# Small value and key-value products of twelve units moved ahead of the next unit's scores in one run, and the masked scores kept in the gate tiles

## The chip, the cores and the metric

One core of a Trainium2 chip runs the whole program. The metric is device time in microseconds, the median of three executions, lower is better. A profile of one execution gives the rows that are read here.

## The reference, cut to what matters

Gated linear attention over 4 batches, 8 heads, 768 positions and 48 channels a head, followed by two feed-forward blocks:

```
f = sigmoid(f_logit)
state = f[t][:, None] * state + outer(k[t], v[t])     # for each batch and head, t = 0..767
y[t]  = q[t] @ state
x  = y.reshape(3072, 384)
xn = x / sqrt(mean(x*x) + 1e-6) * rms_g
x  = (silu(xn @ w_gate) * (xn @ w_val)) @ w_out       # 384 -> 1536 -> 384
out = relu(x @ w_in)**2 @ w_out2                      # 384 -> 2048 -> 384
```

## The kernel before, in words

The time axis is cut into 6 chunks of 128 positions; a chunk of one batch is a **unit**, 24 in all, numbered chunk by chunk, and four units make a **group** of 512 tokens. For each unit VectorE scans the gates from both ends (`scan_b`, `scan_a`), scales k and q by them (`mul_k`, `mul_q`), and TensorE forms the `scores` (k against q, 8 products of 64 rows, into PSUM banks `pa` and `pb`). VectorE masks them (`masked`), TensorE adds the state's part and the masked scores times v into the unit's output y (`attend`, 24 small products), and multiplies k by v (`kv`, 8 small products, not for the last chunk). VectorE adds that to the state of the batch (`state_add`); ScalarE has scaled the state by the chunk's gates (`decay`). k is transposed through DRAM (`k_turn`, `k_back`, `kcopy`), y is normalised (`norm`, `power`, `x_scale`), transposed through DRAM (`x_turn`, `x_back`) and split into a rounded and a remainder half (`x_high`, `x_low`).

The first feed-forward block works on a group at a time in 12 steps. A step has three blocks of 9 large products each of 128x512: G (gate), V (value, into bank `vv`) and O (the output product of the step before, called pending). In between ScalarE makes the silu (`sg`) and the rounded hidden half (`hh`), VectorE multiplies by V and makes the remainder (`hl`). The program is one written order: a step is cut into three **segments**, numbered 3f, 3f+1, 3f+2 in a group of 36. Segment 3f stands after G, 3f+1 after V, 3f+2 after O. In each segment first the functions in `side` are issued (VectorE, ScalarE and DMA work), then the step's own silu, multiplication or remainder, then the functions in `tail` (small TensorE products). Each engine takes its instructions in this order, and SyncE issues all transfers in it.

`plan_unit(u, s)` puts the parts of unit u at segments counted from s, the segment of its scores: `attend` at s + 2, `kv` at s + 6, `mul_q` at s itself. Units 8 to 23 are planned so; the first 8 stand in an order written out by hand. Work on the second block's weights (word operations on VectorE, rounded and remainder halves) is put by a planner into segments where its table of costs finds room; the `room` of a segment grows with the small products in it.

TensorE's banks are eight: `acc0` to `acc2` for O, `g`, `vv`, and `pa`, `pb`, `pc`. Before the change y goes to `pa`, the key-value product to `pb`, the masked scores into tiles of their own (`sm`).

Of the kernel before, what the change touches and what calls it, by code (L numbers as in the profile page):

```python
# [8 lines left out]
F32 = mybir.dt.float32  # L9
# [7 lines left out]
P = 128  # L17
B, H, S, D = 4, 8, 768, 48
C = 128
NCH = S // C  # L20
NPAIR = H // 2
DM = H * D
KT = DM // P
# [4 lines left out]
UG = 4  # L28
# [161 lines left out]
def tile_linear_attention_moe(  # L190
# [11 lines left out]
    nc = tc.nc  # L202
# [4 lines left out]
    def pool(name, stack=main, **kw):  # L207
        return stack.enter_context(tc.tile_pool(name=name, **kw))

    ps = pool("ps", bufs=1, space=PSUM)  # L210
# [5 lines left out]
    ap_ = pool("attn", upper, bufs=2, reuse_waits="tile")  # L216

    units = [(c, b) for c in range(NCH) for b in range(B)]
    NU = len(units) // UG
# [6 lines left out]
    mask = cp.tile([P, C], F32, name="mask")  # L226
# [26 lines left out]
    def flat(x):  # L253
        return x.rearrange("p a t -> p (a t)")


    U = {}
# [74 lines left out]
    def banks(u):  # L332
        return ("pa", "pb", "pc") if u >= UG or u % 2 == 0 else ("acc0", "acc1", "acc2")
# [41 lines left out]
    BL = 4  # L375

    def block_view(x, n):
        return flat(x)[:, 0:BL * n * 32].rearrange("p (b n j) -> p b n j", b=BL, n=n)

    def block_write(u, nm, t):  # L380
        n = t.shape[2]
        U[u][nm] = tc.dram_tile([P, BL, n, 32], F32, name=f"{nm}{u}")
        nc.sync.dma_start(U[u][nm], t)

    def block_read(u, nm, to):
        src = U[u][nm].rearrange("(a i) c n j -> c i a (n j)", a=BL)
        for c in range(BL):
            nc.sync.dma_start(to[32 * c:32 * c + 32].rearrange("i a n j -> i a (n j)"), src[c])
        U[u][nm + "o"] = to
# [15 lines left out]
        U[u]["xg"] = xg  # L405

    def x_turn(u):
        t = block_view(U[u]["q"], KT)
        nc.vector.transpose(
            t.rearrange("p a k i -> p k a i"), U[u]["xg"].rearrange("p (k a j) -> p k a j", k=KT, a=BL),  # L410
        )
        block_write(u, "xd", t)

    def x_back(u):
        block_read(u, "xd", ap_.tile([P, BL, KT, 32], F32, tag="sm", name=f"xo{u}", bufs=4))

    def x_part(t, u):
        return t[:, :, u % UG * C:(u % UG + 1) * C].rearrange("p k (c i) -> p k c i", c=BL)
# [21 lines left out]

    def attend(u):
        c, b = units[u]
        y = ps.tile([P, DM], F32, tag=banks(u)[0], name=f"y{u}")
        sub = [True, True]
        if c:
            for p in range(NPAIR):
                for i in range(2):
                    o = slice(64 * i, 64 * i + 64)
                    nc.tensor.matmul(
                        y[o, p * 2 * D:(p + 1) * 2 * D], U[u]["q"][:, p, o], state[b][:, p],  # L450
                        start=sub[i], stop=False, skip_group_check=True,
                    )
                    sub[i] = False
        for hf in range(2):
            sm = U[u]["sm", hf]
            for j in range(4):
                h = 2 * j + hf
                hs = slice(h * D, (h + 1) * D)
                for i in range(2):
                    o = slice(64 * i, 64 * i + 64)  # L460
                    nc.tensor.matmul(
                        y[o, hs], sm[:, j, o], U[u]["v"][:, hs],
                        start=sub[i], stop=True, skip_group_check=True,
                    )
                    sub[i] = False
        U[u]["y"] = y

    def kv(u):
        c, b = units[u]
        if c == NCH - 1:  # L470
            return
        kvp = ps.tile([P, NPAIR, D], F32, tag=banks(u)[1], name=f"kv{u}")
        for p in range(NPAIR):
            for o in (0, 64):
                h = 2 * p + o // 64
                nc.tensor.matmul(
                    kvp[o:o + D, p], U[u]["ktok"][:, p, o:o + D], U[u]["v"][:, h * D:(h + 1) * D],
                    start=True, stop=True,
                )
        U[u]["kv"] = kvp  # L480
# [269 lines left out]
    side, tail, planned, room = {}, {}, {}, {}  # L750
    TAIL = dict(scores=0.9, attend=1.3, kv=0.3)

    def at(where, s, fn):
        where.setdefault(max(s, NG), []).append(fn)

    starts = {}

    def plan_unit(u, s):
        starts[u] = s
        for k, fns in (  # L760
            (-9, (load_gates,)), (max(-9, starts.get(u - 2, 0) + 7 - s), (load_v,)),
            (max(-9, starts.get(u - 2, 0) + 9 - s), (load_qk,)),
            (-5, (gate,)), (-3, (scan_b, keep_end)), (-1, (scan_a, mul_k)),
            (0, (mul_q, k_turn, decay)), (1, (masked,)), (2, (k_back,)), (3, (norm, power)), (4, (x_scale,)),
            (5, (x_turn, kcopy)), (6, (x_back,)), (7, (state_add,)), (10, (x_high, x_low)),
        ):
            for fn in fns:
                if fn not in (load_gates, load_qk, load_v) or u > 2 * UG:
                    at(side, s + k, lambda fn=fn: fn(u))
                    planned.setdefault(s + k, []).append(fn.__name__)  # L770
        for k, fn in ((0, scores), (2, attend), (6, kv)):
            at(tail, s + k, lambda fn=fn: fn(u))
            room[s + k] = room.get(s + k, 0) + TAIL[fn.__name__]

    NG = 3 * F1
    for gi in range(1, NU - 1):
        for j in range(UG):
            plan_unit((gi + 1) * UG + j, gi * NG + ((4, 11, 18, 24) if gi == 1 else (-3, 6, 15, 24))[j])
    COST = dict(
        scan_b=(1.4, 0), keep_end=(0, 0.2), scan_a=(1.2, 0), mul_k=(0.7, 0), mul_q=(0.7, 0), masked=(1.4, 0),  # L780
        k_turn=(0.7, 0), kcopy=(0, 0.6), gate=(0, 2.2), decay=(0, 1.5), norm=(0, 1.0), x_scale=(0.6, 0), x_turn=(0.6, 0),
        state_add=(0.7, 0), x_high=(0, 0.5), x_low=(0.55, 0),
    )
# [149 lines left out]
    def piece(kind, i):  # L933
# [20 lines left out]
    unit_piece = dict(  # L954
        ld=load_unit, sb=scan_b, en=keep_end, sa=scan_a, mk=mul_k, mq=mul_q, sc=scores, kt=ktrans, kc=kcopy,
        y=attend, kv=kv, de=decay, st=state_add, no=norm, pw=power, nr=norm2, xt=xtrans, xh=xhigh, xl=xlow,
    )
    pair_piece = dict(wl=wload, ws=wscale, wb=wbits_low, wc=wbits_sign, wh=whigh, wz=wlow)
# [469 lines left out]
```

## Time and profile before

| what | before |
|---|---|
| median of 3 runs | 947.48 us (947.04 to 948.22) |
| the profiled execution | 947.26 us, of which the span 945.4 us |
| TensorE busy | 921.7 us, 97% of the span, 5945 products |
| VectorE busy | 644.3 us, 68% |
| ScalarE busy | 487.9 us, 52% |
| share of TensorE in the chain that ended last | 91% |

The span is the time from the first to the last instruction of the profiled execution. A busy TensorE is not one at its peak: the ends of its products are modelled and overlap, so what a stretch costs is read from the start times of its instructions.

### The profile page before, as it was taken

What the parts mean: (1) busy time and instruction counts of PE and PEld (TensorE: products, weight loads), DVE (VectorE), ACT (ScalarE), POOL (GpSimd) and SP (SyncE); (2) the same over time, 40 slices, a digit from 0 to 9 for tenths busy, and PEclk for the clock granted to TensorE, in tenths of its full rate; (3) what the DMA queues carried; (4) which work ended last, traced back from release to release, by engine and by line L of the source; (5) the groups of instructions that cost most, each with busy time, mean ns of one, the idle gap of its engine ahead of it and who ended that gap; (6) DMA issues with size and microseconds to landing.
All of it is one profiled execution on the core that took longest, in us unless ns stands there. A gap on an engine that the chain in (4) does not pass through costs nothing.

```text
span 945.4 us, 15739 instructions
## 1 busy us (share of the span) xinstructions
PE 921.7 (97%) x5945; PEld 810.1 (86%) x5945; DVE 644.3 (68%) x1147; ACT 487.9 (52%) x1020; POOL 31.1 (3%) x54
## 2 busy tenths in 40 slices
PE   7799999989999999999999999999999999999997
PEld 4578887878787888878888889999999999999997
DVE  7899968666767877767754636756775676666552
ACT  6877654545444545444433425556546554655551
POOL 3210000000000000000000000000000000000000
PEclk8999999999999999999999999999999999999999
DMA  9455424565556566545237257540754065305300
GB/s 335 165 202 193 178 86 166 160 193 168 161 163 198 182 202 191 185 151 196 106 121 245 74 196 269 183 149 9 242 160 134 15 228 167 126 25 185 117 26 29
DMA packets 78387, 148.48 MB, mean 157 GB/s; under 512 B 17248, under 2 KB 44000, under 8 KB 78304
## 3 DMA queue, kind: packets, MB, share of 16 engines
q1 hardware_dynamic: 78304, 147.39, 47.3%
q8 instruction: 49, 0.80, 0.4%
q14 instruction: 34, 0.28, 0.1%
HBM read 115.12 MB, written 32.24 MB: 156 GB/s over the span
## 4 chain that ended last, share of the span: by engine, by line
PE 91%; DMA 3%; DVE 2%; ACT 2%; issue 1%; SPq 0%; POOL 0%; DVEq 0%; POOLq 0%; ACTq 0%
PE o L730 7%; PE o L728 7%; PE o L729 7%; PE X L1104 7%; PE Y L1104 6%; PE v L728 5%; PE g L728 5%; PE acc L728 5%; PE acc L729 5%; PE acc L730 5%; PE v L730 5%; PE v L729 5%; PE g L730 5%; PE g L729 5%; PE T L1104 2%; PE R L1104 2%
## 5 line engine op out<-in xcount | busy, mean ns | idle before, releaser
L730 PE MATMUL o<-wb,h 128*128 128x384 f32 x384 | 128.6, 335 | 0.0
L729 PE MATMUL o<-wb,h 128*128 128x384 f32 x384 | 128.3, 334 | 0.0
L728 PE MATMUL o<-wb,h 128*128 128x384 f32 x384 | 128.3, 334 | 0.0
L975 ACT CAST hh<-sg 128x512 fp32r<-128x512 f32 x72 | 44.7, 620 | 110.0 <-DVE sg L972 108.8
L972 DVE TENSOR_TENSOR sg<-v,sg 128x512 f32<-128x512 f32 x72 | 49.6, 688 | 61.6 <-PE v L730 61.5
L1104 PE MATMUL X<-xc,wa 128*128 128x384 f32 x360 | 82.4, 336 | 0.0
L730 PEld LDWEIGHTS o<-wb,h 128*128 128x128 f32 x384 | 72.1, 188 | 0.5
L728 PEld LDWEIGHTS o<-wb,h 128*128 128x128 f32 x384 | 72.1, 188 | 0.0
L729 PEld LDWEIGHTS o<-wb,h 128*128 128x128 f32 x384 | 72.1, 188 | 0.0
L967 ACT ACTIVATE sg<-g 128x512 f32<-128x512 f32 x72 | 42.8, 594 | 54.2 <-PE g L730 53.9
L1104 PE MATMUL Y<-xc,wa 128*128 128x384 f32 x300 | 68.3, 335 | 0.0
L1104 PEld LDWEIGHTS X<-xc,wa 128*128 128x128 f32 x360 | 63.7, 188 | 1.8 <-ACT d L1179 1.2
L1183 DVE TENSOR_TENSOR c<-T,c 128x384 f32<-128x384 f32 x40 | 22.3, 558 | 52.4 <-PE T L1104 43.3
L977 DVE TENSOR_TENSOR hl<-sg,hh 128x512 fp32r<-128x512 f32 x72 | 49.3, 685 | 9.8 <-ACT hh L975 9.8
L1104 PEld LDWEIGHTS Y<-xc,wa 128*128 128x128 f32 x300 | 53.3, 188 | 0.7 <-DVE c L1183 0.6
L1134 DVE TENSOR_TENSOR h<-d,h 128x384 fp32r<-128x384 f32 x60 | 32.8, 554 | 26.2 <-ACT h L1133 26.2
L1133 ACT CAST h<-d 128x384 fp32r<-128x384 f32 x60 | 30.2, 511 | 34.4 <-PE o L730 34.4
L1179 ACT COPY d<-X 128x384 f32<-128x384 f32 x40 | 19.1, 478 | 54.7 <-PE X L1104 54.7
L728 PE MATMUL g<-xh,wh_o 128*128 128x512 f32 x108 | 43.1, 399 | 0.8 <-ACT sg L967 0.8
L728 PE MATMUL v<-xh,wh_g 128*128 128x512 f32 x108 | 43.8, 406 | 0.0
L728 PE MATMUL v<-xh,wh_v 128*128 128x512 f32 x108 | 43.4, 402 | 0.1
L728 PE MATMUL g<-xh,wh_g 128*128 128x512 f32 x108 | 43.2, 400 | 0.0
(192 smaller groups left out, 2237.5 us busy)
## 6 DMA issues: line engine op xcount, KB each, us to landing
wa<-w2d_c SPq DMA_DIRECT2D x100, 384.0 KB, 3.3
raw<-in_w_dram SPq DMA_DIRECT2D x18, 768.0 KB, 4.3
ff<-in_ff_dram SPq DMA_DIRECT2D x20, 516.0 KB, 5.3
qk<-in_qk_dram SPq DMA_DIRECT2D x20, 512.0 KB, 6.4
w2d_c<-ws_c SPq DMA_DIRECT2D x50, 192.0 KB, 2.7
raw_a<-in_w_dram SPq DMA_DIRECT2D x22, 384.0 KB, 4.2
wb<-w2d_b SPq DMA_DIRECT2D x16, 384.0 KB, 3.7
v<-in_vp_dram SPq DMA_DIRECT2D x24, 192.0 KB, 5.6
```

Of the source, the lines that this page charges most:

```text
L728: nc.tensor.matmul(o, lh, rh, start=first, stop=False)
L729: nc.tensor.matmul(o, lh, rl, start=False, stop=False)
L730: nc.tensor.matmul(o, ll, rh, start=False, stop=last)
L967: nc.scalar.activation(dd["s", f], dd["g", f], AF.Silu)
L972: nc.vector.tensor_mul(dd["s", f], dd["v", f], dd["s", f])
L975: nc.scalar.copy(dd["h", f][0], dd["s", f])
L977: nc.vector.tensor_sub(dd["h", f][1], dd["s", f], dd["h", f][0].bitcast(F32))
L1104: nc.tensor.matmul(o, w[a], x[:, b], start=first and n == 0, stop=last and n == 2, skip_group_check=True,)
L1133: nc.scalar.copy(t[:, 0], r)
L1134: later(lambda: nc.vector.tensor_sub(t[:, 1], r, t[:, 0].bitcast(F32)))
L1179: nc.scalar.copy(t, bk[b])
L1183: nc.vector.tensor_add(t, bk[b], t)
```

## The change

For units 12 to 23 `attend` and `kv` leave their own places and stand at e, the segment of the next unit's scores, ahead of these: one run of small products (attend, kv, scores of the next unit) where three stood apart. e is nine segments after s; the first segments of the units move a little so that each e is one that follows O (3f+2). The output y goes to bank `pc` (units 8 and on), the key-value product to `pc` for units 8 to 11 and to `vv`, the bank of the value block, from unit 12 on. The masked scores of units 12 and on are written over the unit's two gate tiles (`r` one segment after the scores, `f` three after), so the next load into these waits for `attend`. `x_turn` writes into a tile of its own, and `mul_q` and `mul_k` stand one segment ahead of the scores for all planned units, `scan_a` two. Work after `attend` (norm, scale, turn) moves with it.

```
-        t = block_view(U[u]["q"], KT)
+        t = ap_.tile([P, BL, KT, 32], F32, tag="xn", name=f"xt{u}")
...
+    def mask_into(u, hf, x):
+        sm = flat(x)[:, 0:4 * C].rearrange("p (j t) -> p j t", j=4)
+        nc.vector.tensor_mul(sm, U[u]["sc", hf], mask.unsqueeze(1).broadcast_to([P, 4, C]))
+        U[u]["sm", hf] = sm
+    def mask_r(u):
+        mask_into(u, 0, U[u]["r"])
+    def mask_f(u):
+        mask_into(u, 1, U[u]["f"])
...
-        y = ps.tile([P, DM], F32, tag=banks(u)[0], name=f"y{u}")
+        y = ps.tile([P, DM], F32, tag="pc" if u >= 2 * UG else banks(u)[0], name=f"y{u}")
...
-        kvp = ps.tile([P, NPAIR, D], F32, tag=banks(u)[1], name=f"kv{u}")
+        kvp = ps.tile([P, NPAIR, D], F32, tag="vv" if u >= 3 * UG else "pc" if u >= 2 * UG else banks(u)[1], name=f"kv{u}")
...
+    def plan_unit(u, s, e=None):
+        far = e is not None
+        y, b = (e, e + 1) if far else (s + 2, s + 3)
+        kv_at, back = (e, e + 4) if far else (s + 6, s + 6)
+        g = -5 if far else -6
+        end = e + 8 if far else s + 10
+        for n, at_ in zip(("gates", "qk", "v"), (e + 1,) * 3 if far else (s + 4, s + 6, s + 7)):
+            free[n, u] = at_
+        plan = [
+            (max(s - 10, free.get(("gates", u - 2), 0)), (load_gates,)),
+            (max(s - 9, free.get(("v", u - 2), 0)), (load_v,)),
+            (max(s - 9, free.get(("qk", u - 2), 0)), (load_qk,)),
+            (s + g, (gate,)), (s + g + 2, (scan_b, keep_end)), (s - 2, (scan_a,)), (s - 1, (mul_k, mul_q)),
+            (s, (k_turn, decay)), (s + 1, (mask_r,) if far else (masked,)), (s + 2, (k_back,)),
+            (s + 3, (mask_f,) if far else ()), (s + 5, (kcopy,)), (kv_at + 1, (state_add,)),
+            (b, (norm, power)), (b + 1, (x_scale,)), (b + 2, (x_turn,)), (back, (x_back,)), (end, (x_high, x_low)),
+        ]
...
-        for k, fn in ((0, scores), (2, attend), (6, kv)):
-            at(tail, s + k, lambda fn=fn: fn(u))
+        for k, fn in ((s, scores), (y, attend), (kv_at, kv)):
+            at(tail, k, lambda fn=fn: fn(u))
...
-            plan_unit((gi + 1) * UG + j, gi * NG + ((4, 11, 18, 24) if gi == 1 else (-3, 6, 15, 24))[j])
+    begin = [NG + x for x in (4, 11, 18, 24)]
+    for gi in range(2, NU - 1):
+        begin += [gi * NG + x for x in (-7 if gi == 2 else -10, -1, 8, 17)]
+    begin.append(begin[-1] + 9)
+    for n in range(len(begin) - 1):
+        plan_unit(2 * UG + n, begin[n], begin[n + 1] if n >= UG else None)
```

On TensorE, before, the small products of units 14 and 15 stand in three places. `y14` is unit 14's attend, `kv14` its key-value product, `sc15` the two score banks of unit 15; `acc`, `g` and `v` are large products of the feed-forward block:

```order
L730 MATMUL acc_2_2_2593<-hh_2_4_2815,wl_o4_891 128x512
L449 MATMUL y14_2910<-state2_99,qk14_2628 64x96 x8
L461 MATMUL y14_2910<-v14_2626,sm14_0_2883 64x48 x8
L461 MATMUL y14_2910<-v14_2626,sm14_1_2885 64x48 x8
L728 MATMUL g_2_6_2935<-xh_1_2_1876,wh_g6_969 128x512
...
L476 MATMUL kv14_3023<-v14_2626,ktok14_2988 48x48 x8
L728 MATMUL v_2_7_3032<-xh_1_2_1876,wh_v7_1055 128x512
...
L341 MATMUL sc15_0_3094<-qk15_2852 128x128
L341 MATMUL sc15_1_3095<-qk15_2852 128x128
```

On TensorE, after the change, the same products of units 14 and 15 (the two rows of scores come four times):

```order
L741 MATMUL acc_2_2_2626<-hh_2_4_2844,wl_o4_891 128x512
L460 MATMUL y14_2912<-state2_99,qk14_2527 64x96 x8
L472 MATMUL y14_2912<-v14_2525,ff14_2523 64x48 x16
L487 MATMUL kv14_2937<-v14_2525,ktok14_2837 48x48 x8
L341 MATMUL sc15_0_2946<-qk15_2765 128x128
L341 MATMUL sc15_1_2947<-qk15_2765 128x128
...
L739 MATMUL g_2_6_2956<-xh_1_2_1877,wh_g6_969 128x512
```

They have moved into one run between O and the next G; of the four borders with large products that the second and the third place had, none is left.

On TensorE, before, around the key-value product of unit 10 and the scores of unit 11, which stand together in both programs, with the engines whose semaphores they wait for:

```order
L476 MATMUL kv10_2161<-v10_1783,ktok10_2117 48x48 [waits PE_49,Activation_49]
L476 MATMUL kv10_2161<-v10_1783,ktok10_2117 48x48 x7
L341 MATMUL sc11_0_2170<-qk11_2032 128x128 [waits DMAHW3_49,DVE_49,PE_49]
L341 MATMUL sc11_1_2171<-qk11_2032 128x128 [waits DVE_49,PE_49]
L341 MATMUL sc11_0_2170<-qk11_2032 128x128
```

On TensorE, after the change, at the same place:

```order
L487 MATMUL kv10_2151<-v10_1785,ktok10_2114 48x48 [waits DVE_49,Activation_49]
L487 MATMUL kv10_2151<-v10_1785,ktok10_2114 48x48 x7
L341 MATMUL sc11_0_2160<-qk11_1954 128x128 [waits DMAHW5_49,DVE_49]
L341 MATMUL sc11_1_2161<-qk11_1954 128x128
L341 MATMUL sc11_0_2160<-qk11_1954 128x128
```

The order is the same, but the key-value product now lies in `pc`, and the second bank of scores (`sc11_1`) waits for VectorE and for TensorE no longer.

On VectorE, before, between the state addition of unit 14 and the transposition of unit 15's k (L319 is `mul_k`, L322 `mul_q`, L316 `scan_a`, L395 `k_turn`, `sg` the product with V, `hl` the remainder):

```order
L492 TENSOR_TENSOR state2_99<-kv14_3023,state2_99 48x4x48 x2
L665 TENSOR_TENSOR ws_c1_3_2995<-ws_c1_3_2995 128x384
L972 TENSOR_TENSOR sg_2_7_3021<-v_2_7_3032,sg_2_7_3021 128x512
L316 SCALAR_TENSOR_TENSOR ff15_2848<-ff15_2848,seed_90 128x516
L319 TENSOR_TENSOR qk15_2852<-qk15_2852,ff15_2848 128x512
L977 TENSOR_TENSOR hl_2_7_3054<-sg_2_7_3021,hh_2_7_3053 128x512
L322 TENSOR_TENSOR qk15_2852<-qk15_2852,ff15_2848 128x512
L395 STREAM_TRANSPOSE ff15_2848<-qk15_2852 128x4x4x32
```

On VectorE, after the change, the same instructions:

```order
L319 TENSOR_TENSOR qk15_2765<-qk15_2765,ff15_2761 128x512
L322 TENSOR_TENSOR qk15_2765<-qk15_2765,ff15_2761 128x512
L995 TENSOR_TENSOR sg_2_5_2872<-v_2_5_2874,sg_2_5_2872 128x512
L395 STREAM_TRANSPOSE ff15_2761<-qk15_2765 128x4x4x32
L721 TENSOR_TENSOR ws_c1_0_2840<-m_a3_2654,ws_c1_0_2840 128x128
L721 TENSOR_TENSOR ws_c1_0_2840<-m_a3_2654 128x128
L1000 TENSOR_TENSOR hl_2_5_2890<-sg_2_5_2872,hh_2_5_2889 128x512
L503 TENSOR_TENSOR state2_99<-kv14_2937,state2_99 48x4x48 x2
L419 TENSOR_TENSOR ff15_2761<-sc15_0_2946,mask_88 128x512
```

`mul_q` has moved ahead of the product with V (`sg`) of the segment before the scores, and the state addition now stands behind the remainder `hl` and ahead of the mask of the next unit.

## Rows read from the trace of the kernel before

**Rows 1.** The page, part 1: busy time, share of the span, instructions

```profile
PE 921.7 (97%) x5945; PEld 810.1 (86%) x5945; DVE 644.3 (68%) x1147; ACT 487.9 (52%) x1020; POOL 31.1 (3%) x54
```

**Rows 2.** Windows, stretch of planned units: us, busy by engine, clock, DMA

```profile
133.00:490.00 357.00, 352.09 (x2499) 285.14 (x2498) 249.37 (x440) 172.20 (x357) 8.78 (x16) 1.00 0.54 173
```

**Rows 3.** Waits of TensorE, whole span: total us, times, longest

```profile
PE sc L341 <- PE g L730: 0.5, 2, 0.2
```

**Rows 4.** Timeline of TensorE, key-value product alone: start us, us, instruction

```profile
304.05 0.39 PE L730 MATMUL g<-xh,wl_g 128*128 128x512 f32 x1
...
305.20 0.39 PE L729 MATMUL v<-xl,wh_g 128*128 128x512 f32 x1
```

**Rows 5.** Timeline of TensorE, scores alone

```profile
310.89 0.39 PE L730 MATMUL g<-xh,wl_o 128*128 128x512 f32 x1
311.21 1.16 PE L341 MATMUL sc<-qk 64*128 64x128 f32 x16
...
312.64 0.39 PE L729 MATMUL v<-xl,wh_v 128*128 128x512 f32 x1
```

**Rows 6.** Timeline of TensorE, a block O and an attend alone

```profile
314.47 0.39 PE L728 MATMUL acc<-hh,wh_o 128*128 128x512 f32 x1
...
316.29 0.39 PE L730 MATMUL acc<-hh,wl_o 128*128 128x512 f32 x1
...
318.67 0.39 PE L729 MATMUL g<-xl,wh_g 128*128 128x512 f32 x1
```

**Rows 7.** Timeline of TensorE, unit 6's key-value product with unit 7's attend

```profile
118.20 0.39 PE L730 MATMUL v<-xh,wl_v 128*128 128x512 f32 x1
118.52 0.56 PE L476 MATMUL kv<-v,ktok 128*48 128x48 f32 x16
118.91 0.85 PE L449 MATMUL y<-state,qk 128*64 128x96 f32 x16
...
120.94 0.39 PE L729 MATMUL acc<-hl,wh_o 128*128 128x512 f32 x1
```

**Rows 8.** Timeline of TensorE, key-value product of unit 10, scores of unit 11

```profile
195.40 0.39 PE L730 MATMUL g<-xh,wl_g 128*128 128x512 f32 x1
195.72 0.56 PE L476 MATMUL kv<-v,ktok 128*48 128x48 f32 x16
196.21 0.49 PE L341 MATMUL sc<-qk 64*128 64x128 f32 x2
199.17 1.13 PE L341 MATMUL sc<-qk 64*128 64x128 f32 x14 [2.47 <-DVE state L492]
...
200.56 0.39 PE L729 MATMUL v<-xl,wh_g 128*128 128x512 f32 x1
```

**Rows 9.** Timeline of TensorE and VectorE, ahead of unit 21's scores

```profile
422.23 0.39 PE L730 MATMUL g<-xh,wl_g 128*128 128x512 f32 x1
...
423.16 0.69 DVE L322 TENSOR_TENSOR qk<-qk,ff 128x512 f32<-128x512 f32 x1
...
423.95 0.79 PE L341 MATMUL sc<-qk 64*128 64x128 f32 x9 [1.33 <-issue]
```

**Rows 10.** Groups of VectorE in 133 to 490 us: count, busy, mean ns

```profile
L972 DVE TENSOR_TENSOR sg<-v,sg 128x512 f32<-128x512 f32 x47 | 32.5, 691 | 38.4 <-PE v L730 38.3
...
L568 DVE SCALAR_TENSOR_TENSOR m_a<-raw_a,m_a 128x768 int32<-128x768 int32 x10 | 9.5, 953 | 0.3
...
L492 DVE TENSOR_TENSOR state<-kv,state 48x192 f32<-48x192 f32 x25 | 8.8, 353 | 2.2 <-PE kv L476 2.1
L395 DVE STREAM_TRANSPOSE ff<-qk 128x512 f32<-128x512 f32 x12 | 8.5, 712 | 0.4
```

**Rows 11.** Windows, behind small products early on, and behind rows 8

```profile
32.00:36.00 4.00, 4.00 (x27) 1.96 (x26) 3.97 (x8) 2.18 (x5) 0.88 (x2) 0.75 0.59 197
...
201.00:204.00 3.00, 3.00 (x15) 2.45 (x14) 1.13 (x2) 0.60 (x2) 0.00 (x0) 1.00 0.82 283
```

**Rows 12.** DMA issues: count, KB each, median us from issue to landing

```profile
ff<-in_ff_dram SPq DMA_DIRECT2D x20, 516.0 KB, 5.3
```

More of the change, by code (lines that the diff above doesn't have):

```diff
@@ L754, in at @@
         where.setdefault(max(s, NG), []).append(fn)
[L756 to L766, printed above, removed]
+    free = {}
@@ new lines, in plan_unit @@
+    def plan_unit(u, s, e=None):
[15 more added lines that the diff above has]
+        ]
+        for k, fns in plan:
@@ L767, in plan_unit @@
             for fn in fns:
                 if fn not in (load_gates, load_qk, load_v) or u > 2 * UG:
-                    at(side, s + k, lambda fn=fn: fn(u))
-                    planned.setdefault(s + k, []).append(fn.__name__)
-        for k, fn in ((0, scores), (2, attend), (6, kv)):
-            at(tail, s + k, lambda fn=fn: fn(u))
-            room[s + k] = room.get(s + k, 0) + TAIL[fn.__name__]
-    NG = 3 * F1
-    for gi in range(1, NU - 1):
-        for j in range(UG):
-            plan_unit((gi + 1) * UG + j, gi * NG + ((4, 11, 18, 24) if gi == 1 else (-3, 6, 15, 24))[j])
+                    at(side, k, lambda fn=fn: fn(u))
@@ new lines, in plan_unit @@
+                    planned.setdefault(k, []).append(fn.__name__)
+        for k, fn in ((s, scores), (y, attend), (kv_at, kv)):
+            at(tail, k, lambda fn=fn: fn(u))
+            room[k] = room.get(k, 0) + TAIL[fn.__name__]
+    NG = 3 * F1
+    begin = [NG + x for x in (4, 11, 18, 24)]
[4 more added lines that the diff above has]
+        plan_unit(2 * UG + n, begin[n], begin[n + 1] if n >= UG else None)
@@ L779, in tile_linear_attention_moe @@
     COST = dict(
-        scan_b=(1.4, 0), keep_end=(0, 0.2), scan_a=(1.2, 0), mul_k=(0.7, 0), mul_q=(0.7, 0), masked=(1.4, 0),
+        scan_b=(1.4, 0), keep_end=(0, 0.2), scan_a=(1.2, 0), mul_k=(0.7, 0), mul_q=(0.7, 0), masked=(1.4, 0), mask_r=(0.7, 0), mask_f=(0.7, 0),
         k_turn=(0.7, 0), kcopy=(0, 0.6), gate=(0, 2.2), decay=(0, 1.5), norm=(0, 1.0), x_scale=(0.6, 0), x_turn=(0.6, 0),
```

## The prediction, made before the changed kernel was run

> **What bounds the kernel now.** The page first: TensorE is busy 97% of the span, VectorE 68%, ScalarE 52% [rows 1]. So a change pays only where it takes time out of TensorE's own sequence, and costs only where it makes TensorE wait. The stretch that the change touches is that of the planned units, 133 to 490 us: TensorE shows 352.1 of 357.0 us busy there at a granted clock of 1.00, the 2.4 GHz level [rows 2]. That looks full, but busy ends are modelled, so I read start times. Eight steps inside one block O take 316.29 - 314.47 = 1.82 us, 0.2275 us a product, 2.05 us a block of nine [rows 6]. Around small products the steps are longer: from the last large product ahead of unit 15's scores to its first scores 311.21 - 310.89 = 0.32 us instead of 0.23 [rows 5]. A change between large and small products therefore costs something each way, and joining runs should save it.
>
> **What the change removes: borders.** I measure a run from the start of the last large product ahead of it to the start of the second large product behind it; two large steps (0.455 us) belong to the large work.
> - Attend alone: 318.67 - 316.29 = 2.38 us [rows 6]. Key-value product alone: 305.20 - 304.05 = 1.15 [rows 4]. Scores alone: 312.64 - 310.89 = 1.75 [rows 5].
> - One joined run exists already, unit 6's key-value product with unit 7's attend: 120.94 - 118.20 = 2.74 [rows 7]. Apart they take 2.38 + 1.15 - 0.455 = 3.075. **A join of these two saves 0.335 us.** Its attend begins 0.39 us after the key-value product did, with no hole between [rows 7]. After the change attend comes first; I take the same price, since both use all 128 rows of the array in both orders.
> - Scores behind a key-value product stand in one place, which then stalls [rows 8]. Up to the first scores it takes 196.21 - 195.40 = 0.81, and from the first scores on a free run takes 312.64 - 311.21 = 1.43 [rows 5]; joined without a stall 2.24, apart 1.15 + 1.75 - 0.455 = 2.445. **A join with scores behind saves 0.205 us.** No row shows scores behind an attend (units 20 to 22 have no key-value product); I take 0.205 there too.
> - Count: units 12 to 19 join attend and key-value product (8), the scores of units 13 to 23 stand behind another small product (11). 8 x 0.335 + 11 x 0.205 = 2.68 + 2.26 = **4.9 us**. Bounds: all 19 at 0.335 give 6.4; none worth anything gives 0.
>
> **What it removes: stalls.**
> - Unit 10's key-value product lies in bank `pb`, where unit 11's scores go next. Two scores issue, then TensorE waits 2.47 us for the state addition that reads the bank [rows 8]. With the product in `pc` the order shows no such wait. The run took 200.56 - 195.40 = 5.16 us against 2.24 free: **2.9 us**. Lower bound 0 if VectorE held it anyway; but `mul_q` of unit 11, the other thing the scores need, now stands a segment earlier.
> - `mul_q` stands in the same segment as the scores before. For unit 21 it starts at 423.16, takes 0.69, and the scores begin at 423.95, 1.72 us after the last large product instead of 0.32: 1.40 us lost, booked as "issue" but ended by `mul_q` [rows 9]. Two more scores waited 0.5 us in all the same way [rows 3]. After the change `mul_q` is issued ahead of the product with V, and between V's end and the scores TensorE has a block O and an attend, 2.05 + some 1.9 us: **1.9 us** saved, lower bound 0.
>
> **What it adds, at nothing, and what covers it.**
> - The value bank: from unit 12 the key-value product sits in `vv`, and the next V must wait for the state addition. From the start of the key-value product to V TensorE now has 0.49 (to the first scores), 1.43 and a block G of 2.05, some 4.0 us [rows 5, 6, 8]. In the worst row, with the transposition and weight work queued ahead, the addition let the scores go 199.17 - 195.72 = 3.45 us after the product began [rows 8]. Counted from V's end the longest queue that the order shows for these units is the product with V (0.69), the transposition (0.71), three word operations (0.95 at most each), the remainder (about 0.69) and two additions (0.35 each) [rows 10]: 5.7 us, against 2.05 for O, 3.4 for the joined run and 2.05 for G, 7.5. Room of 1.8 us, less what VectorE is late when V ends; nothing charged.
> - Masks in the gate tiles: the gates of unit u + 2 load only after attend of u, and ScalarE's sigmoid work on them stands three blocks later, 6.1 us [rows 6], against a median landing of 5.3 us [rows 12]. Should they land late, silu waits behind them on ScalarE, but the next G needs its bank only after V and O, 4.1 us later.
> - The turned x has its own tile, the second mask stands two segments later; both on VectorE, same count of instructions, off TensorE's path. Transfers are the same in number and size; SyncE's loads move behind attend.
> - The planner puts the weight work later. The last split of an input for the second block still stands ahead of three whole steps, some 18 us, so phase two starts as before.
>
> **Sum.** 4.9 + 2.9 + 1.9 = 9.7 us less. The profiled execution took 947.26 us, 0.22 below the median shown; 947.26 - 9.7 = 937.6. I predict **937.5 us**.
>
> **A rule against it.** The joined run of rows 7 shows weights of an attend following a key-value product on the same 128 rows without a hole, and 0.335 us saved. The Trainium skill, "TensorE: Matmul & The Clock Gate", section "The mechanism" in Part 3, says that a weight load overlaps products in flight only when their row groups differ. By that rule neither kind of join would run on without a pause, the joins would be worth nothing and the time 942.5. Rows 7 disagree for one of the two; no row settles attend followed by scores.
>
> **The rivals.**
> 1. *Joins worth nothing* (what a run costs follows its own loads, not its borders): only the stalls go, 947.3 - 4.8 = 942.5. For it: the scores' first steps stay slow behind a key-value product too (0.205 against 0.335). Against it: rows 7. Chance 0.09.
> 2. *The value bank becomes the wait, slower.* If V stood still for the state addition as the scores of unit 11 did, 2.47 us [rows 8] in each of 8 units, 19.8 us: 937.5 + 19.8 = 957.3. It eats the gain from 1.2 us a unit on, that is if the addition ends over 3 us later than the queue above says. For it: VectorE is the busiest engine after TensorE, 249 of 357 us [rows 2]. Against it: the two sums above. Chance 0.05.
> 3. *The clock.* A run of 3.4 us of small products leaves most of the array idle. After sparse small work early on the granted clock was 0.75 over 4 us, partly the 1.2 GHz level: 1.0 us lost [rows 11]. Eleven joined runs at that price: 948.5, no change. Against it: behind the key-value product, stall and scores of rows 8, some 4.5 us, the clock stayed 1.00 [rows 11]. Chance 0.04.
> 4. *Late gates or a crowded VectorE* hold the scores or the silu in part of the units: half of the gain gone, 942.5 to 945. For it: 5.3 us is only a median, and units 12 and 13 have two blocks, 4.1 us, instead of three [rows 6, 12]. Against it: 4.1 us of slack. Chance 0.07.
>
> **How the numbers follow.** The forecast has 0.75: from 935.0 (all joins at 0.335 give 936.1; another 1 us where ends of other small waits go) to 940. Taking in rival 1 and the lower half of rival 4 the range is 935.0 to 942.6, with about 0.84 of the chance. A measurement of this kernel tells about 0.2%, 1.9 us, from no change. Rivals 1 and 4 are still faster by more than that: faster 0.75 + 0.09 + 0.07 = 0.91; same 0.04, rival 3 with the edges; slower 0.05, rival 2.
>
> **What would show it.** In the profile after: joined runs of 2.38 + 1.15 + 1.75 - 2 x 0.455 - 0.335 - 0.205 = 3.83 us where attend, key-value product and scores stand together, and 3.47 where attend and scores alone do (2.38 + 1.75 - 0.455 - 0.205); unit 11's scores without a wait; scores of units 12 to 23 with no idle time ahead; V behind each joined run starting one step after G. Wrong would be: idle time ahead of V that the state addition ends, a clock below 1.00 after the joined runs, or ScalarE waiting for gates with G idle behind it.

## The result, and the profile after

| | before | after |
|---|---|---|
| median, five runs each, in turn on one chip | 947.48 us (947.04 to 950.25) | 938.55 us (937.19 to 939.01) |
| ratio, 95% interval | | 0.9897 [0.9881, 0.9914] |
| the profiled execution | 947.26 us, span 945.4 | 937.19 us, span 934.7 |

The kernel became 8.9 us faster by the medians, against 937.5 us predicted: the time lies 1.05 us above the number and inside the range. The page of the kernel after, part 1, answers to [rows 1]: 921.7 us of busy TensorE have become 915.9, with the same 5945 products.

```profile
PE 915.9 (98%) x5945; PEld 810.3 (87%) x5945; DVE 640.9 (69%) x1147; ACT 488.6 (52%) x1020; POOL 34.2 (4%) x54
```

The window over the planned units of the kernel after (us, busy by engine, clock, DMA share, GB/s) answers to [rows 2]. TensorE was idle for 4.9 of 357 us there, and is idle for 0.7 of 363 now. Busy ends are modelled, so this says where holes went and not what the borders gave.

```profile
121.00:484.00 363.00, 362.26 (x2583) 298.13 (x2582) 253.81 (x454) 178.23 (x368) 11.95 (x17) 1.00 0.53 166
```

**Where the time came from.** I cut both executions by start times on TensorE: an early part up to the first G of group 2, the planned stretch from there to the last V of the first block, and the rest. The two limits, in the timeline of the kernel before and then of the kernel after:

```profile
134.56 0.39 PE L728 MATMUL g<-xh,wh_g 128*128 128x512 f32 x1
...
564.20 0.39 PE L730 MATMUL v<-xh,wl_v 128*128 128x512 f32 x1
```

```profile
132.25 0.39 PE L739 MATMUL g<-xh,wh_g 128*128 128x512 f32 x1
...
553.12 0.39 PE L741 MATMUL v<-xh,wl_v 128*128 128x512 f32 x1
```

The planned stretch went from 564.20 - 134.56 = 429.64 to 553.12 - 132.25 = 420.87 us: **8.8 us**, nearly all of the difference of the medians. The early part, counted from the first product, is 133.1 us in the profiled execution before and 130.8 after; TensorE's order is the same there in both, and in the ten experiments below it lies anywhere from 130.3 to 133.5, in programs with the order of before (131.7 and 130.7 in the first two) as with that of after. It differs from execution to execution, so I compare kernels by the planned stretch, and by medians only beside it. The rest, from the last V to TensorE's last product, is 375.0 before, 375.7 after, and 374.8 to 375.6 in the experiments. So the two profiled executions differ by 10.1 us and the medians by 8.9.

Inside the planned stretch the account closes. I add up what each run of small products takes, from the last large product ahead to the second behind, less two large steps of 0.2267 us: 65.53 us in 44 runs before, 54.91 us in 25 runs after, 10.62 less. The large products among themselves lost 1.86 us to new waits: 10.62 - 1.86 = 8.76.

A joined run of the kernel after, unit 15's attend and key-value product with unit 16's scores, in the timeline of TensorE:

```profile
286.94 0.39 PE L741 MATMUL acc<-hh,wl_v 128*128 128x512 f32 x1
287.26 0.88 PE L460 MATMUL y<-state,qk 128*64 128x96 f32 x16
287.97 1.09 PE L472 MATMUL y<-v,ff 128*64 128x48 f32 x32
288.88 0.53 PE L487 MATMUL kv<-v,ktok 128*48 128x48 f32 x16
289.35 1.16 PE L341 MATMUL sc<-qk 64*128 64x128 f32 x16
290.44 0.50 PE L739 MATMUL g<-xh,wh_o 128*128 128x512 f32 x1
290.77 0.40 PE L740 MATMUL g<-xl,wh_o 128*128 128x512 f32 x1
```

290.77 - 286.94 = 3.83 us, and all eight such runs take this. Where unit 20's attend and unit 21's scores stand alone, the same stretch reads 399.46 - 395.99 = 3.47 us, as for all three of that kind:

```profile
395.99 0.39 PE L741 MATMUL acc<-hh,wl_o 128*128 128x512 f32 x1
396.31 0.88 PE L460 MATMUL y<-state,qk 128*64 128x96 f32 x16
...
399.46 0.40 PE L740 MATMUL g<-xl,wh_g 128*128 128x512 f32 x1
```

Unit 10's key-value product with unit 11's scores, 5.16 us before [rows 8], takes 195.55 - 193.31 = 2.24 us:

```profile
193.31 0.39 PE L741 MATMUL g<-xh,wl_g 128*128 128x512 f32 x1
193.63 0.56 PE L487 MATMUL kv<-v,ktok 128*48 128x48 f32 x16
194.12 1.16 PE L341 MATMUL sc<-qk 64*128 64x128 f32 x16
...
195.55 0.40 PE L740 MATMUL v<-xl,wh_g 128*128 128x512 f32 x1
```

**The new waits**, in the view of TensorE's waits of the kernel after (us in total, times, longest). No scores of a planned unit are left in it. The first row was 0.8 in one place before; the second is new; the third stood there with the same time, but outside the planned stretch.

```profile
PE g L739 <- ACT sg L990: 1.5, 2, 0.8
...
PE v L739 <- DVE sg L995: 0.2, 1, 0.2
PE acc L740 <- DVE hl L1000: 0.2, 1, 0.2
```

The added 0.7 us stand in the second step of group 2. The timeline there, first of ScalarE, then of TensorE: the silu of the first G (L990) is issued behind `keep_end` (L312), a copy of the scan's last column, and that waits 1.30 us for VectorE's scan. The first product of the next G starts 1.12 us after the product ahead of it instead of 0.23, and the one behind it is late by another 0.11.

```profile
136.48 0.20 ACT L312 COPY ends<-ff 128x4 f32<-128x4 f32 x1 [1.30 <-DVE ff L308]
136.58 0.59 ACT L990 ACTIVATE sg<-g 128x512 f32<-128x512 f32 x1
```

```profile
136.10 0.39 PE L741 MATMUL v<-xh,wl_g 128*128 128x512 f32 x1
137.22 0.50 PE L739 MATMUL g<-xh,wh_o 128*128 128x512 f32 x1 [0.74 <-ACT sg L990]
```

Two more, at 538 and 541 us near the end of the first block, cost 0.50 and 0.44 us by start times: V waits for the product with V of the step before, O for a remainder. In the timeline of VectorE that product (537.73) stands behind two splits of the second block's input (L1115), the first of which waits 0.58 us for ScalarE's rounding, and the remainder (540.46) behind a pair of splits that waits 1.10 us. This is read from the order; no run moves these splits.

```profile
536.79 0.56 DVE L1115 TENSOR_TENSOR xc<-xs,xc 128x384 fp32r<-128x384 f32 x1 [0.58 <-ACT xc L1114]
...
539.52 1.03 DVE L1115 TENSOR_TENSOR xc<-x,xc 128x384 fp32r<-128x384 f32 x2 [1.10 <-ACT xc L1114]
```

**The value bank** is at its limit in one place, unit 18. The state addition on VectorE runs from 357.13 to 357.85, and V starts at 357.99, 0.14 us later. That is no room left over: in the four experiments in which V came late behind the addition, it did so twelve times in all, and each time it started 0.15 us after the addition's end. Here V still starts one step after the last G product, but its own second product follows 0.31 us later, as behind each of the twelve, and the block takes 0.1 us longer than the usual 2.05. What used the room up stands ahead on VectorE: it waited 1.54 us for ScalarE's rounding of a weight, with the weight work, the remainder and the addition queued behind.

```profile
354.20 0.56 DVE L676 TENSOR_TENSOR ws_c<-ws_c 128x384 fp32r<-128x384 f32 x1 [1.54 <-ACT ws_c L675]
...
357.13 0.72 DVE L503 TENSOR_TENSOR state<-kv,state 48x192 f32<-48x192 f32 x2
```

```profile
354.25 0.53 PE L487 MATMUL kv<-v,ktok 128*48 128x48 f32 x16
...
357.75 0.40 PE L741 MATMUL g<-xh,wl_g 128*128 128x512 f32 x1
357.99 0.47 PE L739 MATMUL v<-xh,wh_g 128*128 128x512 f32 x1
358.30 0.39 PE L740 MATMUL v<-xl,wh_g 128*128 128x512 f32 x1
```

### The profile page after: what moved, and what is told of

The parts are those of the page before. It is cut to its first block, busy times and chain, and to the rows that moved or that the text cites. A ratio compares the mean times of both kernels' runs of the same rounds, so it can differ in the third digit from the quotient of the medians.

```text
span 934.7 us, 15748 instructions
## 1 busy us (share of the span) xinstructions
PE 915.9 (98%) x5945; PEld 810.3 (87%) x5945; DVE 640.9 (69%) x1147; ACT 488.6 (52%) x1020; POOL 34.2 (4%) x54
## 4 chain that ended last, share of the span: by engine, by line
PE 89%; DVE 3%; ACT 2%; DMA 1%; issue 0%; SPq 0%; DVEq 0%; ACTq 0%
PE o L741 7%; PE o L740 7%; PE o L739 7%; PE X L1127 7%; PE Y L1127 5%; PE g L739 5%; PE acc L739 5%; PE v L739 5%; PE acc L740 5%; PE acc L741 5%; PE g L741 5%; PE g L740 5%; PE v L741 5%; PE v L740 5%; PE T L1127 2%; PE sc L341 2%
## 5 line engine op out<-in xcount | busy, mean ns | idle before, releaser
L990 ACT ACTIVATE sg<-g 128x512 f32<-128x512 f32 x72 | 42.8, 595 | 74.0 <-PE g L741 73.8
L739 PE MATMUL acc<-hh,wh_o 128*128 128x512 f32 x108 | 42.8, 396 | 0.0
```

What stands on the lines that cost most here:

```text
L739: nc.tensor.matmul(o, lh, rh, start=first, stop=False)
L990: nc.scalar.activation(dd["s", f], dd["g", f], AF.Silu)
```

## The experiments

The ten kernels ran in three sessions, with the kernel before at 948.62, 948.31 and 948.31 us in them. "Planned" is the planned stretch of the one profiled execution; 429.64 before, 420.88 after. The small changes to the kernel after can't be told from it by their medians: the intervals of all but three of these overlap its own, 0.9881 to 0.9914 (those of the late `mul_q`, the four reductions and the score bank lie outside). What such a change did is therefore read from its trace. Each edit is made to before or to after as said. Every kernel computes the whole reference.

### One part alone: the bank (on before)

```
-        kvp = ps.tile([P, NPAIR, D], F32, tag=banks(u)[1], name=f"kv{u}")
+        kvp = ps.tile([P, NPAIR, D], F32, tag="pc" if u >= 2 * UG else banks(u)[1], name=f"kv{u}")
```

> The kernel before, with one edit: the key-value products of units 8 and on lie in bank pc instead of pb. If the wait of unit 11's scores for the state addition was the price that the prediction put on it, 2.9 us go: about 944.6, and those scores show no idle time. Rival: VectorE holds these scores anyway, by its queue; then 947.5 and the wait only changes its name.

Measured: 943.52 us, ratio 0.9951 [0.9938, 0.9965]; planned 426.66, 2.98 less; the small runs cost 2.92 less, all of it in the run of unit 10's key-value product and unit 11's scores, which takes 2.24 us as in the kernel after. The term for the bank is right. The median fell by 5.1, more than the planned stretch accounts for; the early part, where this edit changes nothing, was 1.4 us shorter than in the profiled execution before, and why the median fell further is open.

### One part alone: `mul_q` a segment earlier (on before)

```
-            (-5, (gate,)), (-3, (scan_b, keep_end)), (-1, (scan_a, mul_k)),
-            (0, (mul_q, k_turn, decay)), ...
+            (-5, (gate,)), (-3, (scan_b, keep_end)), (-2, (scan_a,)), (-1, (mul_k, mul_q)),
+            (0, (k_turn, decay)), ...
```

> The kernel before, with one edit: scan_a two segments and mul_q one segment ahead of the scores. If mul_q was what the scores of units 15, 18 and 21 waited for, 1.9 us go, and up to 0.8 more at units 8 and 9: 944.8 to 945.6, with leads of 0.32 us ahead of all scores but unit 11's. Rival: VectorE is late as a whole, and the wait moves to the product with V or to the remainder: 947.5.

Measured: 943.96 us, ratio 0.9957 [0.994, 0.9974]; planned 427.39, 2.25 less. The small runs cost 3.12 less: 0.34 of it because the stall of unit 11's scores became shorter, 2.78 because every other run of scores now starts 0.32 us after the last large product. The prediction counted 1.9 for units 15, 18 and 21; units 8 and 9 had lost 0.65 and 0.15 too. Some 0.9 us of this was lost again elsewhere, behind the stall that is left, as TensorE's timeline shows (the median fell by 4.7, again more than the planned stretch):

```profile
192.95 0.48 PE L341 MATMUL sc<-qk 64*128 64x128 f32 x2
195.00 1.44 PE L341 MATMUL sc<-qk 64*128 64x128 f32 x14 [1.56 <-DVE state L492]
...
196.96 0.63 PE L729 MATMUL v<-xl,wh_g 128*128 128x512 f32 x1
197.39 0.63 PE L730 MATMUL v<-xh,wl_g 128*128 128x512 f32 x1
```

The large steps are 0.43 us long here, nearly twice the usual, and the granted clock of this stretch (the number behind the five engines) is 0.50, the 1.2 GHz level:

```profile
196.50:198.00 1.50, 1.50 (x4) 1.21 (x5) 0.91 (x2) 0.00 (x0) 0.00 (x0) 0.50 0.87 266
```

### Undoing one join: attend a segment ahead of the run (on after)

```
-        for k, fn in ((s, scores), (y, attend), (kv_at, kv)):
+        for k, fn in ((s, scores), (y - far, attend), (kv_at, kv)):
```

> The changed kernel with attend of units 12 to 23 one segment earlier, behind V, so that block O stands between it and the key-value product; these and the scores stay joined. If the border is what pays, 8 x 0.335 + 3 x 0.205 = 3.3 us come back: about 941.9. Rival: what pays is that the small products stand late, behind work that is done, and the joining is worth nothing: 938.6.

Measured: 940.14 us, ratio 0.9915 [0.9896, 0.9935]. The small runs cost 58.20 - 54.91 = 3.29 us more, as 8 x 0.335 + 3 x 0.205 = 3.30 says. The planned stretch grew by 2.37 only, since the two late waits at 538 and 541 us don't occur in this kernel; that is one reason why the time lies below the 941.9 expected. Each join is worth what the sum says of it; rival 1 (joins worth nothing) has no room left.

### The order inside the run: scores first (on after)

```
-            at(tail, k, lambda fn=fn: fn(u))
+            tail.setdefault(k, []).insert(0 if fn is scores else len(tail[k]), lambda fn=fn: fn(u))
```

> The changed kernel with the next unit's scores ahead of attend and key-value product in the joined run. If a border's price depends only on which two forms meet, in either order, a joined run still costs 3.38 us over its large products, and the time is that of the changed kernel, 938.6. Rival: the scores lose 0.13 us only where they follow another form, and the run costs 3.25: 11 x 0.13 = 1.4 us less; or the later key-value product leaves the state addition too little room and V waits, at least 1 us more.

Measured: 939.81 us, ratio 0.9913 [0.9894, 0.9931]; planned 423.54, 2.66 more than after. Six of the eight full runs and two of the three short ones take 3.83 and 3.47 us as before: the borders cost the same in either order. The other three waited for `mul_q`; the waits view has

```profile
PE sc L341 <- DVE qk L322: 2.5, 3, 1.6
```

and the worst of them reads so, on VectorE and then on TensorE. A remainder (`xl`) stood waiting 3.41 us for ScalarE, and `mul_k` and `mul_q` behind it:

```profile
243.81 0.56 DVE L438 TENSOR_TENSOR xl<-xo,xh 128x384 fp32r<-128x384 f32 x1 [3.41 <-ACT xh L434]
...
244.89 0.69 DVE L322 TENSOR_TENSOR qk<-qk,ff 128x512 f32<-128x512 f32 x1
```

```profile
243.63 0.39 PE L741 MATMUL acc<-hh,wl_v 128*128 128x512 f32 x1
245.63 1.16 PE L341 MATMUL sc<-qk 64*128 64x128 f32 x16 [1.60 <-DVE qk L322]
```

With attend and key-value product in front, some 2.1 us of TensorE work cover this wait. That cover is a gain of the order chosen, beside that of the borders.

### `mul_q` back in its old segment (on after)

```
-            ... (s - 2, (scan_a,)), (s - 1, (mul_k, mul_q)),
-            (s, (k_turn, decay)), ...
+            ... (s - 1, (scan_a, mul_k)),
+            (s, (mul_q, k_turn, decay)), ...
```

> The changed kernel with scan_a and mul_q put back by one segment, to where they stood before. If the place of the joined run, behind block O and attend, is what shields the scores, units 12 and on lose nothing and only units 8 and 9 get back up to 0.8 us: 938.6 to 939.4. Rival: the earlier mul_q is what saved the 1.9 us, and they come back: 940.5 or more.

Measured: 941.06 us, ratio 0.9933 [0.9915, 0.9952]; planned 423.11, 2.23 more. Ten of the eleven runs with an attend ahead kept their length, one was 0.08 longer. Unit 12's scores, which stand alone, lost 1.63, booked as "issue" as unit 21's were [rows 9]; they begin where `mul_q` ends, on VectorE and TensorE:

```profile
208.10 0.65 DVE L322 TENSOR_TENSOR qk<-qk,ff 128x512 f32<-128x512 f32 x1
```

```profile
206.91 0.39 PE L741 MATMUL acc<-hh,wl_o 128*128 128x512 f32 x1
208.85 1.16 PE L341 MATMUL sc<-qk 64*128 64x128 f32 x16 [1.56 <-issue]
```

V now waited for the state addition, 0.82 us at the worst by start times. The time is the rival's, but for another reason, and both theories hold in part: in a joined run the attend ahead covers `mul_q` in either place; of the five planned scores without one, unit 12's need the earlier place, unit 8's lost 0.08 us and the other three nothing. That V waits is a cost of the later place that neither theory named.

### Late state additions: one and four idle reductions ahead of each (on after)

```
+        if u >= 3 * UG:
+            for _ in range(1):
+                nc.vector.tensor_reduce(idle, floor.rearrange("p a t -> p (a t)"), axis=mybir.AxisListType.X, op=ALU.min)
```

The second kernel has `range(4)`. The reductions read a constant, and nobody reads what they write.

> The changed kernel with one idle reduction on VectorE, some 0.6 us, ahead of each state addition of units 12 to 19. After the change the additions end 0.15 to 2.44 us ahead of V's start; only units 18 (0.15) and 19 (0.46) have less than 0.6: 0.6 us in all, about 939.2. Rival: VectorE's queue is what sets the pace and every delay is paid, 8 x 0.6 = 4.8 us: 943.4.

> The changed kernel with four idle reductions on VectorE, some 2.4 us, ahead of each state addition of units 12 to 19. By the slack of each unit (1.66, 1.16, 2.44, 2.44, 2.44, 1.21, 0.15 and 0.46 us) V waits 0.7 + 1.2 + 1.2 + 2.3 + 1.9 = 7.4 us in all: about 946. Rival: nothing waits, since V's bank comes free in time: 938.6; or every delay is paid in full, 19 us: 958.

Measured: one reduction 938.61 us, ratio 0.9905 [0.9888, 0.9922], planned 1.36 more, V's waits for the addition, 0.9 in two units by the view and 1.4 by start times. The units are 13 and 18, not 18 and 19: at unit 13 VectorE was already 1.1 us later than in the kernel after, behind a remainder that waited 2.20 us for ScalarE. Four reductions 946.32 us, ratio 0.998 [0.9967, 0.9994], planned 8.29 more. The waits view of the second, and V of unit 18 in its timeline:

```profile
PE v L745 <- DVE state L509: 7.4, 5, 2.6
```

```profile
360.92 0.53 PE L488 MATMUL kv<-v,ktok 128*48 128x48 f32 x16
...
367.43 0.47 PE L745 MATMUL v<-xh,wh_g 128*128 128x512 f32 x1 [2.61 <-DVE state L509]
367.74 0.40 PE L746 MATMUL v<-xl,wh_g 128*128 128x512 f32 x1
```

From the key-value product to V unit 18 now takes 367.43 - 360.92 = 6.51 us, 2.77 more than the 3.74 of the kernel after, and four reductions of 0.69 us each (from this trace) are 4 x 0.69 = 2.76: V pays the delay in full, as it must where no room is left. The view books 2.61 of it, since it counts idle time from the modelled end of the product ahead. The mechanism of rival 2 exists; in the kernel after it lacked only the lateness.

### The key-value product of units 12 to 19 in a score bank instead (on after)

```
-        ... tag="vv" if u >= 3 * UG else "pc" if u >= 2 * UG else banks(u)[1], ...
+        ... tag="pb" if u >= 3 * UG else "pc" if u >= 2 * UG else banks(u)[1], ...
```

> The changed kernel with the key-value products of units 12 to 19 in bank pb instead of vv, ahead of the scores that use pb. The scores then wait for the state addition in each of 8 joined runs. In the profile after the change the addition ends 0.98 to 3.28 us after the key-value product starts, of which 0.5 us is the product: stalls of 0.4 to 2.7 us, some 10 us in all, about 949. Rival: the bank is of no account in a joined run: 938.6.

Measured: 954.01 us, ratio 1.0075 [1.0047, 1.0103], slower than before; planned 436.40, 15.5 more than after, where some 10 were expected. The waits view, and the worst run (unit 18 and 19) on TensorE:

```profile
PE sc L341 <- DVE state L503: 10.5, 8, 2.8
```

```profile
365.07 0.49 PE L341 MATMUL sc<-qk 64*128 64x128 f32 x2
368.36 1.13 PE L341 MATMUL sc<-qk 64*128 64x128 f32 x14 [2.80 <-DVE state L503]
...
370.01 0.63 PE L740 MATMUL g<-xl,wh_g 128*128 128x512 f32 x1
370.44 0.63 PE L741 MATMUL g<-xh,wl_g 128*128 128x512 f32 x1
```

This is the stall of rows 8 in all eight units. The small runs cost 14.35 us more, 3.85 more than the view books as waits, some 0.5 a unit. That it is lost because two scores run out and the rest start anew is argued from the rows, not tested. Behind this one, and only here, six large steps took 0.43 us, at the lower clock (0.50). The bank that the joined run's key-value product goes to decides between a gain and a loss.

### The silu ahead of the copy of the scan's end (on after)

```
-            (s + g, (gate,)), (s + g + 2, (scan_b, keep_end)), ...
+            (s + g, (gate,)), (s + g + 2, (scan_b,)), (s + g + 3, (keep_end,)), ...
```

> The changed kernel with the copy of the scan's last column (keep_end) one segment later for the planned units, so that the first silu of the second group no longer stands behind it on ScalarE. In the profile after the change the second G of that group waits 0.9 us for that silu, a wait that the profile before does not have; if the copy, which waits for VectorE's scan, is what holds it, some 1.0 us goes: about 937.6. Rival: the sigmoid work itself is late, and the wait stays: 938.6.

Measured: 937.94 us, ratio 0.9889 [0.9871, 0.9906]; planned 419.89, 0.99 less than after. The wait of G for the silu is back at the one of before, and the cause of the first new wait is shown. The waits at the end of the block stayed (0.59 and 0.44 us by start times).

```profile
PE g L739 <- ACT sg L990: 0.8, 1, 0.8
```

### The same join for units 8 to 11 too (on after)

```
-        kvp = ps.tile([P, NPAIR, D], F32, tag="vv" if u >= 3 * UG else "pc" if u >= 2 * UG else banks(u)[1], ...
+        kvp = ps.tile([P, NPAIR, D], F32, tag="vv" if u >= 2 * UG else banks(u)[1], ...
...
-        far = e is not None
-        y, b = (e, e + 1) if far else (s + 2, s + 3)
-        kv_at, back = (e, e + 4) if far else (s + 6, s + 6)
+        far = u >= 3 * UG
+        y, b = e, e + 1
+        kv_at, back = e, e + 4
...
-        end = e + 8 if far else s + 10
+        end = min(e + 8, u // UG * NG - 1)
...
-    begin = [NG + x for x in (4, 11, 18, 24)]
+    begin = [NG + x for x in (5, 11, 17, 23)]
...
-        plan_unit(2 * UG + n, begin[n], begin[n + 1] if n >= UG else None)
+        plan_unit(2 * UG + n, begin[n], begin[n + 1])
```

The masks of these four units stay in tiles of their own (`far` now chooses the gate tiles and the times that hang on them, no longer the joined run).

> The changed kernel with units 8 to 11 joined as well: attend and key-value product at the next unit's scores, first segments 5, 11, 17, 23 of their group, key-value products in vv; their masks stay in tiles of their own. By the price of the borders 4 x 0.335 + 3 x 0.205 = 1.95 us more are saved: about 936.6. Rival: six segments a unit leave VectorE too little room, V waits for the state addition, and it is 938.6 or slower.

Measured: **935.89 us**, ratio 0.9863 [0.984, 0.9886], the lowest median of the kernels tried; planned 418.38, 2.50 less than after. Its interval still touches that of the kernel after. The joins gave 4 x 0.335 + 3 x 0.205 = 1.95 less in the small runs, as the prices of the others say. Of this 0.64 was lost in one run, whose key-value product waits in the value bank for the multiplication that reads V, and 0.84 where one V waited for a state addition; the late silu is gone, and of the waits at the end 0.1 us is left. Its waits view:

```profile
PE v L739 <- DVE state L503: 0.6, 1, 0.6
PE kv L487 <- DVE sg L995: 0.4, 1, 0.4
```

This kernel and the one with the moved copy were not joined in one; in this one the copy makes nobody wait.

## Why the prediction was right, point by point

- **Joins, 4.9 us:** right; 4.94 was the sum, 4.92 measured. The runs took 3.83 and 3.47 us as written down; against the parts apart that is 8 x 0.539 + 3 x 0.204 = 4.92. What was taken on trust, the order attend ahead of key-value product and scores behind an attend, holds, and the experiment with the order reversed shows that borders cost the same either way. The Trainium skill ("TensorE: Matmul & The Clock Gate", "The mechanism" in Part 3) has a rule by which weights are loaded beside products in flight only into other row groups; taken alone it would have made the joins worth nothing, though the same section also names a background weight buffer that a load may go to. The traces disagree with the rule taken alone, in all eight joins of attend and key-value product, which both use all 128 rows (0.335 us less each), and in all eleven with scores behind (0.205). The rows of before did so already: large products, each with a load of its own of 0.19 us into the same 128 rows, follow each other every 0.2275 us [rows 6].
- **Bank of unit 10, 2.9 us:** right. 2.92 alone, and 5.16 to 2.24 us in the kernel after. Of the two causes offered, the bank did it; the earlier `mul_q` alone left 1.56 us of the wait.
- **`mul_q`, 1.9 us:** the mechanism is right, the term too small. It counted units 15, 18 and 21 and overlooked units 8 and 9, though the waits view of before had 0.6 us of this as scores waiting for `mul_q`; by start times it is worth 2.78 us.
- **What it adds, at nothing:** three parts. The value bank cost only 0.1 us, but the room of 1.8 us was mis-sized: from the addition's end to V, less the 0.15 us that V takes to start behind it, it was nothing at unit 18, 0.3 us at unit 19, and over 1.0 in the other six. That so little was lost is in part luck. One of the two estimates took some 4.0 us from the key-value product's start to V, measured 357.99 - 354.25 = 3.74: the 1.43 us of the scores run to the second product of G, and the block G of 2.05 counts that step again. The other, a longest queue of 5.7 us, added up VectorE's own work and left out what it waits for ScalarE in between, 1.54 us at unit 18; it only said in passing that VectorE may be late. Late gates didn't appear. What did appear is a silu behind a copy that waits for a scan, 1.0 us, and a late product and remainder at the end of the block, 0.9 us: rival 4's kind of loss at about a third of its size. Of the first the cause is shown. Of the second the timeline names the splits of the second block's input, and the experiments show only that it comes and goes with the order elsewhere (it is absent with attend apart, with `mul_q` late, and nearly so with units 8 to 11 joined). The prediction had let the planner's later work cost nothing because phase two starts as before; it does, and the product with V stands behind that work all the same.
- **The sum:** 4.92 + 2.92 + 2.78 - 1.86 = 8.76 us where 9.7 was said. Two errors, 0.9 us of stalls overlooked and 1.9 us of waits unforeseen, of opposite sign, leave it 0.9 short; that the two partly cancel is luck.
- **The clock** (rival 3): 1.00 in the window over the planned stretch. Steps of 0.23 us follow every joined run.

## What to carry to other kernels

Read the price of a change between kinds of products from start times, as the last large product ahead to the second behind, and joins can be summed before anything is built. When products are joined, place in front those whose inputs are ready, and let them cover the inputs of the last; then ask in which bank each result lies, and who must read it before the next writer. A gap between that reader's end and the writer's start is room only beyond what the handover itself takes, 0.15 us here. Leave no copy that waits for a far engine ahead of the step's own work in an in-order queue.

## What was not expected of the hardware

The joined run keeps TensorE on small products for 290.44 - 287.26 = 3.2 us, and the large steps behind it are at full speed. A run of small products with a wait inside it can end at half the clock: behind 1.56 us of waiting in one experiment and 2.80 in another the steps were 0.43 us. But the 2.47 us of rows 8, also between two scores and the rest, left it at 1.00 [rows 11], as did seven of the eight stalled runs with the score bank and the 2.61 us ahead of V, between large products. What decides between these stays open.

A V that waited for the state addition started 0.15 us after its end in twelve cases of twelve, and its second product came 0.31 us behind the first instead of 0.23.
